# Centroid products of an attention kernel: float32 operands in place of two float32r parts

## The chip, the cores and the metric

The kernel runs on one core of a Trainium2 chip. The metric is the device time of the whole program in microseconds, the median of three runs. Five engines work side by side, each on its own list of instructions: PE (TensorE, matmuls; its weight loads are shown as PEld), DVE (VectorE), ACT (ScalarE), POOL (GpSimd), and SP, which only issues transfers here.

## The reference

Attention over 2 batches of 8 heads (768 positions, 64 wide) in which a query sees only the keys of its own cluster, then two feed-forward layers. What matters here is how a cluster is chosen:

```python
q_n = q / (norm(q) + 1e-6);  k_n = k / (norm(k) + 1e-6);  c_n = centroids / (norm(centroids) + 1e-6)
q_assign = argmax(einsum('bhsd,hcd->bhsc', q_n, c_n), axis=-1)      # 16 centroids per head
k_assign = argmax(einsum('bhsd,hcd->bhsc', k_n, c_n), axis=-1)
mask = q_assign[:, :, :, None] == k_assign[:, :, None, :]
attn = softmax(where(mask, q @ k.T / sqrt(64), -1e9));  x = attn @ v
x = g1(x @ w1_in) @ w1_out;  out = g2(x @ w2_in) @ w2_out           # 1536 tokens, 512 and 2048 wide
```

A query's length does not change which centroid wins, so the kernel normalises the centroids alone.

## The kernel before

Two heads make a pair; there are eight pairs, 0 to 7. Matmuls take float32r, a shortened float32, so the kernel splits each float32 value into a high part (rounded to float32r) and a low part (the rest) and adds the products of the parts.

The attention is a pipeline of slots, 24 for each pair. In a slot (`run_slot`) PE transposes three 128x128 blocks of the softmax numerators p into a PSUM tile pt (L527), makes half a row block of scores s (L475, L478), and multiplies earlier blocks with v (L545, L546). ACT copies pt into its high part phi (L530) and takes exponentials (L493). DVE takes row maxima nm (L484) and the low part plo of pt (L535), and only then is pt's PSUM bank free. Three PSUM banks (`ps_t`) serve pt and all other short-lived PSUM tiles in turn.

`prep_pair(i)` prepares pair i while pair i-1 is in its slots. Each `yield` ends its share of a slot. In its order:

- for q (s=0) and k (s=1) and each half hf: three transposes into ptq (L329), ACT copies ptq to SBUF as t32 (L337), and one slot later (`qk_parts`) POOL makes from t32 the high part th and the low part tl (L301, L302). For pairs 2 to 7 (`i >= NDVE`) t32 is a tile with two buffers, so that the third and fourth copy use the buffers of the first and second; pairs 0 and 1 write th directly.
- over four further slots the products with the centroids: for each block of 128 positions two matmuls, with th and with tl as the stationary operand, and 64 moving columns that hold the high and the low parts of the pair's centroids (L367, L368). One step of a slot is three blocks, so six matmuls.
- `sum_dots`, once for q and once for k: DVE adds the products with the two centroid parts and writes dots to SBUF (L356).
- then, a slot or more apart, the winner: maximum mx (L414), comparison eq (L416), a product on POOL (L418), and two more steps on DVE (L423, L425), which make a one-hot code in dots.

From about the middle of the attention on, `pump` adds one step of the conversion of the feed-forward weights every eighth slot (wx and w, L139 to L158, most of them on DVE). POOL's list in the slots of a preparation holds the parts of v (L439, L440), of the attention's result (L584, L585) and of t32, in an order fixed when the program is built. In slots 18 and on the order on PE, ACT, DVE and POOL is the order in which the code issues (`manual_schedule`); before that a scheduler orders it. The feed-forward layers follow, 2,304 matmuls of 512 columns.

Of the kernel before, what the change touches and what calls it, by code (L numbers as in the profile page):

```python
# [8 lines left out]
F32 = mybir.dt.float32  # L9
# [5 lines left out]
ALU = mybir.AluOpType  # L15
AX = mybir.AxisListType
PSUM = bass.MemoryType.PSUM

P = 128
# [8 lines left out]
NDVE = 2  # L28
# [4 lines left out]
def attention_moe_moe(  # L33
# [18 lines left out]
    nc = tc.nc  # L52
    B, H, S, D = q.shape
    C = centroids.shape[1]
    NT, DM = out.shape
    DFF = w1_in.shape[1]
    NJ = S // P
    HJ = NJ // 2
    HS = S // 2
    NPAIR = H // 2  # L60
# [33 lines left out]
    xh = cpool.tile([P, NPAIR, NT], F32R, name="xh")  # L94
    xl = cpool.tile([P, NPAIR, NT], F32R, name="xl")
    cn = cpool.tile([P, NPAIR, 2, 2, C], F32R, name="cn")

# [3 lines left out]
    def later(n, f, *args):  # L103
        due.setdefault(now[0] + n, []).append((f, args))
# [85 lines left out]
    with ExitStack() as actx:  # L190
# [42 lines left out]
        def centroid_setup(ct):  # L233
            sq = ct[:, 1]
            nc.vector.tensor_tensor(sq, ct[:, 0], ct[:, 0], ALU.mult)
            ss = ap.tile([P, 5], F32, tag="css", name="css")
            nc.vector.tensor_reduce(ss[:, 0:1], sq, AX.X, ALU.add)
            y = ss[:, 1:2]
            sq = nc.scalar.activation(y, ss[:, 0:1], AF.Sqrt)
            with tc.issue_after(ins(sq)):  # L240

                nc.scalar.activation(ss[:, 4:5], desc[:, 0:1], AF.Exp, scale=0.0)
            for _ in range(2):
                nc.vector.tensor_scalar(y, y, 1e-30, None, ALU.max)
                nc.vector.reciprocal(ss[:, 2:3], y)
                nc.vector.scalar_tensor_tensor(
                    ss[:, 3:4], ss[:, 0:1], ss[:, 2:3], y, ALU.mult, ALU.add)
                nc.vector.tensor_scalar(y, ss[:, 3:4], 0.5, None, ALU.mult)
            nc.vector.tensor_scalar(ss[:, 2:3], y, 1e-6, None, ALU.add)
            nc.vector.reciprocal(ss[:, 3:4], ss[:, 2:3])  # L250
            cd = ap.tile([P, HS], F32, tag="xt1", bufs=2, name="cd")[:, :P].rearrange(
                "p (r d) -> p r d", r=2)
            for r in range(2):
                nc.vector.tensor_scalar(cd[:, r], ct[:, 0], ss[:, 3:4], None, ALU.mult)
            nc.vector.memset(cn.bitcast(F32), 0.0)
            return cd

        def centroid_parts(cd):
            pc = ps_t.tile([P, HS], F32, tag="t", name="pc")
            mm = nc.tensor.transpose(pc[:, :P], cd.rearrange("p r d -> p (r d)"), ident)  # L260
            run_idle(NIDLE[1], ins(mm))
            pcv = pc[:, :P].rearrange("p (g h c) -> p g h c", h=2, c=C)
            for r in range(2):
                rows = slice(r * D, (r + 1) * D)
                nc.scalar.activation(cn[rows, :, 0, r], pcv[rows, :, r], AF.Copy)
                nc.vector.tensor_tensor(
                    cn[rows, :, 1, r], pcv[rows, :, r], cn[rows, :, 0, r].bitcast(F32),
                    ALU.subtract)

        prepped = {}  # L270

# [4 lines left out]
        def prep_pair(i):  # L276
# [7 lines left out]
            else:  # L284
# [2 lines left out]
            st = [[ap.tile([P, 2, S], F32R, tag=f"st{n}", bufs=3, name=f"st{n}_{i}_{h}")  # L287
                   for n in range(2)] for h in range(2)]
            prepped[i] = [None, st]

            def copy(dst, src):
                nc.sync.dma_start(dst.bitcast(F32), src.bitcast(F32))
# [31 lines left out]
            for s in range(2):  # L324
                sc = D ** -0.5 if s == 0 else 1.0
                for hf in range(2):
                    pt = ps_t.tile([P, HS], F32, tag="t", name=f"ptq{i}_{s}_{hf}")
                    for jj in range(HJ):
                        tr = nc.tensor.transpose(  # L329
                            pt[:, jj * P:(jj + 1) * P],  # L330
                            t[:, s, hf * HJ + jj].rearrange("p h d -> p (h d)"), ident)
                    cols = slice(hf * HS, (hf + 1) * HS)
                    if i < NDVE:
                        t32 = th[:, s, cols]
                    else:
                        t32 = ap.tile([P, HS], F32, tag="t32", bufs=2, name=f"t32_{i}_{s}_{hf}")
                    nc.scalar.activation(t32, pt, AF.Copy, scale=sc)  # L337
                    later(1, qk_parts, s, cols, t32, pt, sc)
                    yield
                later(1, stack, s)  # L340
                if i == 0 and s == 0:
                    with tc.issue_after(ins(tr)):
                        centroid_parts(cd)
                yield
# [13 lines left out]
                    pd.rearrange("p j t h c -> p j (h c) t"), AX.X, ALU.add)  # L358

            rhs = cn[:, hp].rearrange("p t h c -> p (t h c)")  # L360
            for s in range(2):
                pd = ps_t.tile([P, NJ, 2, 2, C], F32, tag="t", name=f"pd{i}_{s}")
                for j in range(NJ):
                    cols = slice(j * P, (j + 1) * P)
# [45 lines left out]
            else:  # L410
                dv = dots.rearrange("p j s h c -> p (j s h) c")
                mb = mx.unsqueeze(2).to_broadcast([P, G, C])
                yield
                nc.vector.tensor_reduce(mx, dv, AX.X, ALU.max)  # L414
                yield
                nc.vector.tensor_tensor(eq, dv, mb, ALU.is_ge)  # L416
                yield
                nc.gpsimd.tensor_tensor(  # L418
                    eq, eq, desc.unsqueeze(1).to_broadcast([P, G, C]), ALU.mult)
# [369 lines left out]
```

## Time and profile before

| | |
|---|---|
| three runs | 816.03 us median (815.66 to 819.19) |
| profiled execution | span 818.6 us from the first to the last instruction; no time of its own is listed |
| PE busy | 797.4 us, 97% of the span |
| PEld, DVE, ACT, POOL busy | 82%, 77%, 49%, 35% |
| attention, then feed-forward | to about 283 us, then 536 us |
| mean granted clock of TensorE | 0.991 |

The span is 0.6 us below the slowest of the three runs and 2.6 us above their median. A matmul's record begins when it starts to stream and its end is modelled, so that records overlap; how long the engine needs for one in a row of its kind is read from start to start.

### The profile page before, as it was taken

How to read it: one execution, taken by the hardware profiler on the slowest of the kernel's cores; microseconds unless marked ns; L12 is line 12 of the kernel's file. 1: busy time of each engine (PE TensorE's matmuls, PEld its weight loads, DVE VectorE, ACT ScalarE, POOL GpSimd, SP SyncE). 2: the span in 40 equal slices, each digit the busy share in tenths (PEclk: the TensorE clock that was granted, in tenths of full speed). 3: DMA queues.
4: the chain of work that ended last, by engine and by line, in shares of the span. 5: the costliest groups of instructions: out<-in, count | busy, mean ns of one | idle time of the engine just before them, and what ended most of it. 6: DMA issues, size and time to landing. Idle time of an engine off the chain costs nothing.

```text
span 818.6 us, 11285 instructions
## 1 busy us (share of the span) xinstructions
PE 797.4 (97%) x4042; PEld 670.6 (82%) x4042; DVE 629.7 (77%) x957; ACT 400.3 (49%) x762; POOL 282.6 (35%) x425
## 2 busy tenths in 40 slices
PE   8899999999999999999999999999999999999998
PEld 5789988889888877888888888888888888888886
DVE  6878978968899787777977777898876987755552
ACT  3688878767788665443434333323444233222220
POOL 3347558574674532222221112332231122111110
PEclk9999999988999999999999999999999999999999
DMA  7875553565440103213121313112122221000012
GB/s 155 192 147 121 134 126 88 119 154 108 97 89 32 52 2 103 92 63 103 52 91 64 102 52 104 52 54 100 52 70 86 61 86 59 1 1 0 14 50 91
DMA packets 48183, 65.97 MB, mean 81 GB/s; under 512 B 27904, under 2 KB 32640, under 8 KB 48128
## 3 DMA queue, kind: packets, MB, share of 16 engines
q1 hardware_dynamic: 47984, 65.22, 29.5%
q8 instruction: 32, 0.52, 0.3%
q14 instruction: 23, 0.19, 0.1%
q10 hardware_dynamic: 144, 0.03, 0.0%
HBM read 43.02 MB, written 3.15 MB: 56 GB/s over the span
## 4 chain that ended last, share of the span: by engine, by line
PE 76%; DVE 10%; POOL 6%; ACT 4%; issue 2%; DMA 1%; SPq 0%; POOLq 0%; ACTq 0%; DVEq 0%
PE y L699 11%; PE y L700 11%; PE y L701 11%; PE h L701 10%; PE h L699 10%; PE h L700 10%; PE pt L527 4%; DVE plo L535 3%; DVE nm L484 3%; PE s L475 2%; PE s L478 2%; PE o L546 2%; PE o L545 2%; ACT phi L530 1%; PE pd L368 1%
## 5 line engine op out<-in xcount | busy, mean ns | idle before, releaser
L657 POOL TENSOR_SCALAR gh<-g 128x512 fp32r<-128x512 f32 x96 | 71.5, 745 | 278.0 <-DVE g L688 157.4
L699 PE MATMUL h<-xh,w 128*128 128x512 f32 x384 | 151.4, 394 | 0.5 <-DVE g L674 0.5
L700 PE MATMUL h<-xl,w 128*128 128x512 f32 x384 | 151.4, 394 | 0.0
L701 PE MATMUL h<-xh,w 128*128 128x512 f32 x384 | 151.3, 394 | 0.0
L535 DVE TENSOR_TENSOR plo<-pt,phi 128x384 fp32r<-128x384 f32 x192 | 99.6, 547 | 16.6 <-ACT phi L530 15.8
L530 ACT ACTIVATE phi<-pt 128x384 fp32r<-128x384 f32 x192 | 93.2, 494 | 36.2 <-PE pt L527 34.4
L484 DVE TENSOR_REDUCE nm<-s 128x1 f32<-128x768 f32 x96 | 91.0, 948 | 19.8 <-PE s L478 18.8
L527 PE MATMUL pt<-ident,p 128*128 128x128 f32 x576 | 98.5, 279 | 7.8 <-DVE plo L535 5.8
L684 ACT ACTIVATE p<-h,mone 128x512 f32<-128x512 f32 x48 | 33.1, 690 | 130.0 <-DVE m L683 129.6
L493 ACT ACTIVATE p<-s,nm 128x768 f32<-128x768 f32 x96 | 86.6, 902 | 8.8 <-DVE nm L484 7.8
L661 DVE TENSOR_TENSOR gl<-g,gh 128x512 fp32r<-128x512 f32 x96 | 71.6, 746 | 20.0 <-POOL gh L657 15.3
L699 PEld LDWEIGHTS h<-xh,w 128*128 128x128 f32 x384 | 71.9, 187 | 18.4 <-DVE g L674 1.0
L701 PEld LDWEIGHTS h<-xh,w 128*128 128x128 f32 x384 | 71.8, 187 | 17.7
L527 PEld LDWEIGHTS pt<-ident,p 128*128 128x128 f32 x576 | 69.9, 141 | 20.0 <-issue 4.2
L700 PEld LDWEIGHTS h<-xl,w 128*128 128x128 f32 x384 | 71.9, 187 | 17.5
L475 PE MATMUL s<-st,st 128*128 128x384 f32 x192 | 81.6, 425 | 2.5 <-ACT p L493 2.3
L139 ACT ACTIVATE wx<-wraw 128x1024 f32<-128x1024 f32 x32 | 36.5, 1140 | 95.5 <-DMA wraw<-in_moe_w_out_dram 47.7
L699 PE MATMUL y<-gh,w 128*128 128x512 f32 x192 | 74.9, 390 | 1.3 <-POOL w L155 1.3
L700 PE MATMUL y<-gl,w 128*128 128x512 f32 x192 | 74.8, 390 | 0.0
L700 PE MATMUL y<-w,gh 128*128 128x512 f32 x192 | 74.8, 390 | 0.0
L699 PE MATMUL y<-w,gh 128*128 128x512 f32 x192 | 74.7, 389 | 0.0
L738 DVE TENSOR_TENSOR acc<-y,acc 128x512 f32<-128x512 f32 x72 | 49.2, 685 | 33.1 <-PE y L701 33.1
(120 smaller groups left out, 1636.3 us busy)
## 6 DMA issues: line engine op xcount, KB each, us to landing
wraw<-in_moe_w_in_dram SPq DMA_DIRECT2D x16, 1024.0 KB, 5.1
wraw<-in_moe_w_out_dram SPq DMA_DIRECT2D x16, 1024.0 KB, 4.9
st<-t SPq DMA_DIRECT2D x24, 192.0 KB, 4.3
st<-th SPq DMA_DIRECT2D x9, 384.0 KB, 4.0
st<-tl SPq DMA_DIRECT2D x18, 192.0 KB, 4.0
st<-th SPq DMA_DIRECT2D x18, 192.0 KB, 4.3
nat<-in_q_dram SPq DMA_DIRECT2D x8, 384.0 KB, 5.1
nat<-in_k_dram SPq DMA_DIRECT2D x8, 384.0 KB, 5.8
```

The costliest lines, as they stand in the source:

```text
L475: nc.tensor.matmul(s[:, step, :HS], qt[:, 0, cols], kt[:, 0, kc], start=True, stop=False)
L484: nc.vector.tensor_reduce(nm, s[:, :, :HS], AX.XY, ALU.max, negate=True)
L493: nc.scalar.activation(p, s[:, :, :HS], AF.Exp, bias=nm, accum_out=dens[u][:, jj, 0:1])
L527: nc.tensor.transpose(ps[:, jj * P:(jj + 1) * P], p[:, kt * P:(kt + 1) * P], ident)
L530: nc.scalar.activation(hi, ps, AF.Copy)
L535: nc.vector.tensor_tensor(lo, ps, hi.bitcast(F32), ALU.subtract)
L657: nc.gpsimd.tensor_scalar(hi, g, 1.0, 0.0, ALU.mult, ALU.add)
L661: nc.vector.tensor_tensor(lo, g, hi.bitcast(F32), ALU.subtract)
L699: nc.tensor.matmul(o, lh, rh, start=first, stop=False)
L700: nc.tensor.matmul(o, lh, rl, start=False, stop=False)
L701: nc.tensor.matmul(o, ll, rh, start=False, stop=last)
L738: nc.vector.tensor_tensor(a, po, a, ALU.add)
```

## The change

For pairs 2 to 7 the products with the centroids become float32 products: the stationary operand is t32 itself, the moving one is `cn32`, 32 columns of float32 centroids (high part plus low part). One matmul stands where two stood (72 where there were 144), all 12 blocks of q and k go into one PSUM tile pd32, and the sum of parts is not needed: mx and eq read pd32 from PSUM. t32 gets four buffers. `cn32` is cleared and filled once by POOL at the start. th and tl are still made; the scores need them. Pairs 0 and 1 are as before.

```diff
--- before.py
+++ after.py
@@ -94,6 +94,7 @@
     xh = cpool.tile([P, NPAIR, NT], F32R, name="xh")
     xl = cpool.tile([P, NPAIR, NT], F32R, name="xl")
     cn = cpool.tile([P, NPAIR, 2, 2, C], F32R, name="cn")
+    cn32 = cpool.tile([P, NPAIR, 2, C], F32, name="cn32")
 
 
 
@@ -253,6 +254,7 @@
             for r in range(2):
                 nc.vector.tensor_scalar(cd[:, r], ct[:, 0], ss[:, 3:4], None, ALU.mult)
             nc.vector.memset(cn.bitcast(F32), 0.0)
+            nc.gpsimd.memset(cn32, 0.0)
             return cd
 
         def centroid_parts(cd):
@@ -266,6 +268,15 @@
                 nc.vector.tensor_tensor(
                     cn[rows, :, 1, r], pcv[rows, :, r], cn[rows, :, 0, r].bitcast(F32),
                     ALU.subtract)
+            later(6, centroid_sum)
+
+        def centroid_sum():
+
+            for r in range(2):
+                rows = slice(r * D, (r + 1) * D)
+                nc.gpsimd.tensor_tensor(
+                    cn32[rows, :, r], cn[rows, :, 0, r].bitcast(F32),
+                    cn[rows, :, 1, r].bitcast(F32), ALU.add)
 
         prepped = {}
 
@@ -287,6 +298,8 @@
             st = [[ap.tile([P, 2, S], F32R, tag=f"st{n}", bufs=3, name=f"st{n}_{i}_{h}")
                    for n in range(2)] for h in range(2)]
             prepped[i] = [None, st]
+
+            t32s = {}
 
             def copy(dst, src):
                 nc.sync.dma_start(dst.bitcast(F32), src.bitcast(F32))
@@ -333,7 +346,8 @@
                     if i < NDVE:
                         t32 = th[:, s, cols]
                     else:
-                        t32 = ap.tile([P, HS], F32, tag="t32", bufs=2, name=f"t32_{i}_{s}_{hf}")
+                        t32 = ap.tile([P, HS], F32, tag="t32", bufs=4, name=f"t32_{i}_{s}_{hf}")
+                    t32s[(s, hf)] = t32
                     nc.scalar.activation(t32, pt, AF.Copy, scale=sc)
                     later(1, qk_parts, s, cols, t32, pt, sc)
                     yield
@@ -358,7 +372,19 @@
                     pd.rearrange("p j t h c -> p j (h c) t"), AX.X, ALU.add)
 
             rhs = cn[:, hp].rearrange("p t h c -> p (t h c)")
-            for s in range(2):
+            pd32 = None
+            if i >= NDVE:
+
+                pd32 = ps_t.tile([P, NJ, 2, 2 * C], F32, tag="t", name=f"pd{i}")
+                for s in range(2):
+                    for j in range(NJ):
+                        jj = j % HJ
+                        nc.tensor.matmul(
+                            pd32[:, j, s], t32s[(s, j // HJ)][:, jj * P:(jj + 1) * P],
+                            cn32[:, hp].rearrange("p h c -> p (h c)"), start=True, stop=True)
+                        if jj == HJ - 1:
+                            yield
+            for s in range(2 if i < NDVE else 0):
                 pd = ps_t.tile([P, NJ, 2, 2, C], F32, tag="t", name=f"pd{i}_{s}")
                 for j in range(NJ):
                     cols = slice(j * P, (j + 1) * P)
@@ -410,10 +436,11 @@
             else:
                 dv = dots.rearrange("p j s h c -> p (j s h) c")
                 mb = mx.unsqueeze(2).to_broadcast([P, G, C])
+                dp = dv if pd32 is None else pd32.rearrange("p j s (h c) -> p (j s h) c", c=C)
                 yield
-                nc.vector.tensor_reduce(mx, dv, AX.X, ALU.max)
+                nc.vector.tensor_reduce(mx, dp, AX.X, ALU.max)
                 yield
-                nc.vector.tensor_tensor(eq, dv, mb, ALU.is_ge)
+                nc.vector.tensor_tensor(eq, dp, mb, ALU.is_ge)
                 yield
                 nc.gpsimd.tensor_tensor(
                     eq, eq, desc.unsqueeze(1).to_broadcast([P, G, C]), ALU.mult)
```

Where the instructions stand now, at three places of the preparation of pair 4 (its copies t32, its products, its winner). The rows are in the order of the engine; in brackets the engines whose signal an instruction waits for; a wait that an earlier one implies is not listed. Lines of the changed kernel are higher by 13 to 27.

ACT before, the four copies t32 (`t_4_s_hf`) with the copies phi and exponentials p between them:

```order
L337 ACTIVATE t_4_0_0_1586<-ptq_0_0_1582 128x384 [waits PE_49]
L530 ACTIVATE phi_3_1592<-pt_3_1588 128x384 [waits PE_49,Activation_49]
L337 ACTIVATE t_4_0_1_1603<-ptq_0_1_1599 128x384 [waits PE_49]
L530 ACTIVATE phi_4_1611<-pt_4_1607 128x384 [waits PE_49,Activation_49]
L493 ACTIVATE p_1624,den_1537<-s_1560,nm_1605 128x768 [waits DVE_49]
L530 ACTIVATE phi_5_1635<-pt_5_1631 128x384 [waits PE_49,Activation_49]
L337 ACTIVATE t_4_1_0_1653<-ptq_1_0_1649 128x384 [waits PE_49,Activation_49,Pool_49]
L530 ACTIVATE phi_0_1661<-pt_0_1657 128x384 [waits PE_49]
L493 ACTIVATE p_1672,den_1671<-s_1614,nm_1655 128x768 [waits DVE_49]
L337 ACTIVATE t_4_1_1_1682<-ptq_1_1_1678 128x384 [waits PE_49,Activation_49,Pool_49]
L530 ACTIVATE phi_1_1688<-pt_1_1684 128x384 [waits PE_49]
L530 ACTIVATE phi_2_1703<-pt_2_1699 128x384 [waits PE_49]
```

and in the changed kernel:

```order
L351 ACTIVATE t_4_0_0_1560<-ptq_0_0_1556 128x384 [waits PE_49]
L557 ACTIVATE phi_3_1566<-pt_3_1562 128x384 [waits PE_49,Activation_49]
L351 ACTIVATE t_4_0_1_1577<-ptq_0_1_1573 128x384 [waits PE_49]
L557 ACTIVATE phi_4_1585<-pt_4_1581 128x384 [waits PE_49,Activation_49]
L520 ACTIVATE p_1598,den_1511<-s_1534,nm_1579 128x768 [waits DVE_49]
L557 ACTIVATE phi_5_1609<-pt_5_1605 128x384 [waits PE_49,Activation_49]
L351 ACTIVATE t_4_1_0_1627<-ptq_1_0_1623 128x384 [waits PE_49]
L557 ACTIVATE phi_0_1635<-pt_0_1631 128x384 [waits PE_49]
L520 ACTIVATE p_1646,den_1645<-s_1588,nm_1629 128x768 [waits DVE_49,Pool_49]
L351 ACTIVATE t_4_1_1_1656<-ptq_1_1_1652 128x384 [waits PE_49]
L557 ACTIVATE phi_1_1662<-pt_1_1658 128x384 [waits PE_49,Activation_49]
L557 ACTIVATE phi_2_1677<-pt_2_1673 128x384 [waits PE_49,Activation_49]
```

The order is the same. The third and the fourth copy waited for POOL and now wait for PE alone. The second p lists POOL now, for its buffer den, which POOL read for the last time some 24 slots earlier; before, the copy's wait implied it.

PE before, the first step of products (`pd`) and the transposes and scores around it:

```order
L546 MATMUL o_1617<-plo_5_1636,vv_991 128x384
L367 MATMUL pd_0_1727<-cn,th_1576 128x64 [waits Activation_49]
L368 MATMUL pd_0_1727<-cn,tl_1577 128x64 [waits Pool_49]
L367 MATMUL pd_0_1727<-cn,th_1576 128x64
L368 MATMUL pd_0_1727<-cn,tl_1577 128x64
L367 MATMUL pd_0_1727<-cn,th_1576 128x64
L368 MATMUL pd_0_1727<-cn,tl_1577 128x64
L527 MATMUL pt_3_1734<-ident,p_1538 128x128 [waits DVE_49,PE_49]
L527 MATMUL pt_3_1734<-ident,p_1567 128x128
L527 MATMUL pt_3_1734<-ident,p_1624 128x128
L475 MATMUL s_1706<-st_2_1_541,st_2_1_540 128x384
L478 MATMUL s_1706<-st_2_1_541,st_2_1_540 128x384
```

and in the changed kernel:

```order
L573 MATMUL o_1591<-plo_5_1610,vv_980 128x384
L382 MATMUL pd_1701<-cn_103,t_4_0_0_1560 128x32 [waits Activation_49]
L382 MATMUL pd_1701<-cn_103,t_4_0_0_1560 128x32 x2
L554 MATMUL pt_3_1705<-ident,p_1512 128x128 [waits DVE_49,PE_49]
L554 MATMUL pt_3_1705<-ident,p_1541 128x128
L554 MATMUL pt_3_1705<-ident,p_1598 128x128
L502 MATMUL s_1680<-st_2_1_545,st_2_1_544 128x384
L505 MATMUL s_1680<-st_2_1_545,st_2_1_544 128x384
L382 MATMUL pd_1701<-cn_103,t_4_0_1_1577 128x32 x3
```

Three rows stand where six stood, in the same slot; the waits for POOL on the products of this and the next step are gone. The wait of the first row, for ACT, stays, as does that of pt for DVE.

DVE before, from the first sum of parts to the comparison:

```order
L356 TENSOR_REDUCE dots_1726<-pd_0_1727 128x6x32
L484 TENSOR_REDUCE nm_1798<-s_1758 128x1 [waits PE_49]
L535 TENSOR_TENSOR plo_5_1784<-pt_5_1779,phi_5_1783 128x384 [waits DVE_49,Activation_49]
L535 TENSOR_TENSOR plo_0_1805<-pt_0_1800,phi_0_1804 128x384 [waits DVE_49,Activation_49]
L356 TENSOR_REDUCE dots_1726<-pd_1_1772 128x6x32
L414 TENSOR_REDUCE mx_1818<-dots_1726 128x24 [waits DVE_49]
L484 TENSOR_REDUCE nm_1832<-s_1807 128x1 [waits PE_49]
L535 TENSOR_TENSOR plo_1_1825<-pt_1_1820,phi_1_1824 128x384 [waits Activation_49]
L535 TENSOR_TENSOR plo_2_1839<-pt_2_1834,phi_2_1838 128x384 [waits Activation_49]
L416 TENSOR_TENSOR eq_1819<-dots_1726,mx_1818 128x384 [waits DVE_49]
```

and in the changed kernel:

```order
L511 TENSOR_REDUCE nm_1758<-s_1726 128x1 [waits PE_49]
L562 TENSOR_TENSOR plo_5_1747<-pt_5_1742,phi_5_1746 128x384 [waits DVE_49,Activation_49]
L562 TENSOR_TENSOR plo_0_1765<-pt_0_1760,phi_0_1764 128x384 [waits DVE_49,Activation_49]
L441 TENSOR_REDUCE mx_1777<-pd_1701 128x24
L511 TENSOR_REDUCE nm_1791<-s_1767 128x1 [waits PE_49]
L562 TENSOR_TENSOR plo_1_1784<-pt_1_1779,phi_1_1783 128x384 [waits DVE_49,Activation_49]
L562 TENSOR_TENSOR plo_2_1798<-pt_2_1793,phi_2_1797 128x384 [waits DVE_49,Activation_49]
L443 TENSOR_TENSOR eq_1778<-pd_1701,mx_1777 128x384 [waits DVE_49]
```

The two sums of parts (L356) are gone; mx and eq (now L441, L443) stand at the places of L414 and L416 and read pd. PSUM banks: before, pd_0 and pd_1 each held a bank from their first product to their sum; now pd32 holds one from its first product to eq.

## Rows read from the trace of the kernel before

**Rows 1.** The page, busy time of the engines and count of their instructions.

```profile
PE 797.4 (97%) x4042; PEld 670.6 (82%) x4042; DVE 629.7 (77%) x957; ACT 400.3 (49%) x762; POOL 282.6 (35%) x425
```

**Rows 2.** Stretches: length, busy PE, PEld, DVE, ACT, POOL, granted clock, DMA share, GB/s.

```profile
19.00:179.00 160.00, 151.79 (x1037) 139.06 (x1036) 135.39 (x238) 123.48 (x278) 99.56 (x154) 1.00 0.58 129
179.00:190.00 11.00, 11.00 (x47) 10.82 (x46) 5.96 (x12) 3.97 (x9) 1.82 (x4) 0.54 1.04 244
```

**Rows 3.** Timeline of PE, pair 7: start, duration, what; in brackets idle and releaser.

```profile
216.56 0.34 PE L546 MATMUL o<-plo,vv 128*128 128x384 f32 x1
216.74 0.19 PE L367 MATMUL pd<-cn,th 128*128 128x64 f32 x1
...
216.88 0.28 PE L367 MATMUL pd<-cn,th 128*128 128x64 f32 x1
...
217.33 0.55 PE L527 MATMUL pt<-ident,p 128*128 128x128 f32 x3
217.63 0.42 PE L475 MATMUL s<-st,st 128*128 128x384 f32 x1
```

**Rows 4.** Waits in the attention: us in total, times, longest.

```profile
ACT t L337 <- POOL tl L302: 5.4, 4, 1.6
...
ACT t L337 <- POOL t L302: 3.1, 3, 1.4
```

**Rows 5.** Timeline, first product steps: PE in pairs 3 and 4, DVE in 3.

```profile
77.20 0.33 PE L546 MATMUL o<-plo,vv 128*128 128x384 f32 x1
...
78.66 0.52 PE L527 MATMUL pt<-ident,p 128*128 128x128 f32 x3 [0.21 <-DVE plo L535]
...
108.78 0.33 PE L546 MATMUL o<-plo,vv 128*128 128x384 f32 x1
...
110.10 0.52 PE L527 MATMUL pt<-ident,p 128*128 128x128 f32 x3 [0.21 <-DVE plo L535]
...
77.96 1.02 DVE L535 TENSOR_TENSOR plo<-pt,phi 128x384 fp32r<-128x384 f32 x2 [0.81 <-ACT phi L530]
```

**Rows 6.** Timeline, pair 5: PE, then DVE.

```profile
140.71 0.33 PE L546 MATMUL o<-plo,vv 128*128 128x384 f32 x1
...
142.56 0.52 PE L527 MATMUL pt<-ident,p 128*128 128x128 f32 x3 [0.21 <-DVE plo L535]
...
140.57 0.90 DVE L143 TENSOR_SCALAR wx<-wx 128x1024 int32<-128x1024 int32 x1
141.85 1.02 DVE L535 TENSOR_TENSOR plo<-pt,phi 128x384 fp32r<-128x384 f32 x2 [0.39 <-ACT phi L530]
```

**Rows 7.** Timeline, pair 6: ACT, then PE, then DVE.

```profile
172.51 0.49 ACT L337 ACTIVATE t<-ptq 128x384 f32<-128x384 f32 x1 [1.63 <-POOL tl L302]
...
172.02 0.34 PE L546 MATMUL o<-plo,vv 128*128 128x384 f32 x1
173.06 0.55 PE L329 MATMUL ptq<-ident,nat 128*128 128x128 f32 x3 [0.70 <-ACT t L337]
...
177.34 0.52 PE L527 MATMUL pt<-ident,p 128*128 128x128 f32 x3 [0.26 <-DVE plo L535]
...
175.20 1.52 DVE L158 TENSOR_TENSOR w<-wx,w 128x1024 fp32r<-128x1024 f32 x1
176.65 1.01 DVE L535 TENSOR_TENSOR plo<-pt,phi 128x384 fp32r<-128x384 f32 x2
```

**Rows 8.** Timeline after pair 5's products: DVE, then PE.

```profile
149.16 0.55 DVE L356 TENSOR_REDUCE dots<-pd 128x192 f32<-128x384 f32 x1
149.74 0.55 DVE L414 TENSOR_REDUCE mx<-dots 128x24 f32<-128x384 f32 x1
...
151.07 1.01 DVE L535 TENSOR_TENSOR plo<-pt,phi 128x384 fp32r<-128x384 f32 x2
...
150.74 0.49 PE L527 MATMUL pt<-ident,p 128*128 128x128 f32 x3
...
151.77 0.52 PE L527 MATMUL pt<-ident,p 128*128 128x128 f32 x3 [0.18 <-DVE plo L535]
```

## The prediction

> **What bounds the kernel now.** I read the busy times of the page first: PE is busy for 797.4 of 818.6 us [rows 1], so only what PE does or waits for can move the time much. The stretches come next. The change lies in the attention, and in its 160 us from 19 to 179 PE is busy 151.8 us, DVE 135.4, ACT 123.5, POOL 99.6, all at full clock; then follow 11 us at a mean granted clock of 0.54, between the levels of 2.4 and 1.2 GHz [rows 2]. So PE leads, DVE is close behind, and there are some microseconds of waiting to look for. The timeline of PE shows them: five of the six preparations that the change touches (pairs 3 to 7) have a late transposition pt right behind the first product step. In the undisturbed step the last product with v (L546) starts at 216.56, the products at 216.74 and pt at 217.33: 0.77 us from L546 to pt [rows 3]. In pair 3 it is 78.66 - 77.20 = 1.46 us, in pair 4 110.10 - 108.78 = 1.32 us [rows 5].
>
> The waits tell where this begins. ACT's copies t32 waited 5.4 + 3.1 = 8.5 us for POOL's low parts [rows 4]: the third copy needs the buffer that POOL still reads. ACT works in order, so phi behind the copy is late, then plo on DVE, then the PSUM bank that pt needs. PE's wait is therefore put down to DVE, though POOL caused it.
>
> **The products themselves.** One now takes 0.1125 us (the last four of a step, 216.88 to 217.33), although its 64 columns stream in far less: 384 columns of the product before took 0.18 us, 216.56 to 216.74 [rows 3]. So what sets the pace is the change of the 128 stationary columns, which each matmul brings. Each float32 product does the work of two old ones. No row shows one. Bounds: if it needed one load and one pass, as a float32 transposition does (three in 0.30 us, 217.33 to 217.63), 72 products would take 72 x 0.10 against 144 x 0.1125 now, 7.2 - 16.2 = -9.0 us. If it needed four loads, 72 x 0.45 = 32.4, +16.2 us. I take two loads with a matmul each, and so no change: the built program holds 4,042 weight loads and 4,042 matmuls, as many as before [rows 1], so that 72 products stand as 144 loads and 144 matmuls. The moving side agrees: a float32 transposition streams 128 columns in 0.10 us, where float32r streams 384 in 0.18, 0.06 for 128; float32 columns take nearly twice as long, and 32 of them take what 64 took. So half the matmul rows in the listing buy PE nothing.
>
> The Trainium skill, "FP8 and Floating Point Precision", section "TensorE Precision Notes", says that true FP32 takes four passes through the array, one for each pairing of high and low halves. Read as four loads, its sum would be 16.2 us more; read as two loads whose matmul streams both halves of the moving operand, it is mine. The transposition row fits the second reading for the moving side, and no row here shows the loads.
>
> **The copies.** With four buffers the third and fourth copy wait for PE alone, and the 8.5 us of ACT's waiting go. What PE gets of it is less, because DVE is late next:
>
> - Pairs 3 and 4: pt comes 0.69 and 0.55 us earlier (1.46 and 1.32 less 0.77). In pair 3 DVE sat idle 0.81 us for phi ahead of the plo that held pt [rows 5], so that plo can come as much earlier, and nothing takes the wait's place; pair 4 has no weight step either. 1.24 us.
> - Pair 5: 142.56 - 140.71 = 1.85, so 1.08 us late. But a weight step (L143, 0.90 us from 140.57) stands on DVE ahead of plo. It ends at 141.47. The two plo take 1.02 us together, the first about 0.55 (an estimate; they overlap a little), so it ends at 142.02 [rows 6]. pt follows 0.15 us later, as at 151.77 after a first plo begun at 151.07 [rows 8]: at 142.17, a gain of 0.39. Pair 7 has the same rows 71.4 us later: 0.39.
> - Pair 6: the transpositions of q and k at 173.06 go back to 172.02 + 0.18 = 172.20 (ACT's 1.63 us for POOL was in their way), 0.86 us. On DVE L158, 1.52 us long, moves with them from 175.20 to 174.34 and ends at 175.86, the first plo at 176.41, and pt comes at 176.56 where it was 177.34: 0.78 [rows 7].
> - Pair 2: a scheduler has moved its products by a few rows; the copies have little to gain there. I take 0, with pair 4's 0.55 us to either side.
>
> Together 1.24 + 0.78 + 0.78 = 2.8 us. If DVE's weight steps did not hold pt, pairs 5 and 7 would give 1.08 each, 0.69 more, and pair 6 up to its L158, 1.52 more: 2.9 us, the good end.
>
> **The sums of parts.** Twelve on DVE go. The first of each pair lies before an idle stretch and gives nothing. The second, 149.16 to 149.74, stands at the head of a stretch in which DVE works without a pause and PE waits for plo (151.77, [rows 8]): 0.58 us. Against it stands the longer hold of the bank: pd32 keeps it until eq, so that the transposition at 150.74 has only two banks. It waits for the plo that comes at 151.07, now 150.49, done at 151.04, so that pt starts at 151.19, 0.45 us late. That takes the place of the wait at 151.77, about as long: on PE the stretch itself gains next to nothing, 0.05 us in each of pairs 2 to 4 as an estimate. In pairs 5 to 7 weight steps keep DVE behind for longer, so the 0.58 us reach PE at the next wait, less about 0.13 for the row maximum whose scores come later: 3 x 0.45. Together 1.5 us. If the wait for the bank and the old one both stay, it is 0.
>
> **Nothing else.** mx takes 0.55 us from SBUF and the sum took 0.55 from PSUM [rows 8], so reading pd32 costs nothing; eq has the same size. POOL's clearing and two additions come once, at the start; POOL is the least busy engine, 35% [rows 1], and PE wants their result in pair 2 only. One load of k on SP moves behind four transfers; it is needed a pair later.
>
> **The sum.** 2.8 + 1.5 = 4.3 us. Its rows come from an execution with a span of 818.6, 2.6 above the median of 816.03; I take it from the median: 811.7 us. Own range 808.8 (the 2.9 us more) to 814.0 (nothing from the sums, 2 us from the copies).
>
> **Rivals.**
>
> A, the clock does not fall. The 11 us at 0.54 cost 11 x 0.46 = 5.1 us [rows 2]. They begin 1.7 us after the last of pair 6's late starts on PE (177.34, [rows 7]), and these shrink. For it: pairs 3 to 5, with smaller waits, lie in the stretch at full clock [rows 2]. Against it: pair 6 still waits over a microsecond by my own count, and the median may hold less of the fall than the profile. 818.6 - 5.1 - 4.3 = 809.2 by the span, 806.7 by the median; 808.
>
> B, the waits come back. DVE, busy for 85% of the attention, holds PE wherever POOL did, and the longer held bank eats the rest. For it: pairs 5 to 7 above. Against it: the idle 0.81 us of pair 3. No gain or one of 1 us: 815.5.
>
> C, the product is dear: four loads, 0.45 us, at each of 72 products on PE, which leads. 811.7 + 16.2 = 827.9. It turns the forecast into a loss from 4.3 / 72 = 0.06 us more a product. Against it: the count of loads.
>
> D, the product is cheap: the load is as short as a transposition's and only one counts. 811.7 - 9.0 = 802.7.
>
> **Chances.** Forecast 0.50, A 0.20, B 0.16, C 0.08, D 0.06. A measurement of this kernel tells from no change what differs by over about 0.5%, 4.1 us: below 811.95 is faster, above 820.1 slower. The forecast lies at that edge, 0.26 faster and 0.24 the same; A and D are faster, B the same, C slower. Faster 0.52, same 0.40, slower 0.08. The range takes in the forecast's, most of A and B: 806.8 to 816.3.
>
> **What would show it.** ACT's copies t32 no longer wait for POOL; L546 to pt in the first step near 0.8 us in pairs 3 and 4, and in pairs 5 to 7 still ended by plo behind a weight step. A product step that takes 0.6 us as before: 144 records of weight loads and a pace of 0.11 us. A step of 1.3 us is C, of 0.3 D. The stretch around 179 to 190 at clock 1.0 is A. Waits of pt for plo one slot earlier than at 151.77 show the bank. Wrong would be a time outside the range, or the right time with the copies still waiting.

## The result: 809.5 us, 0.8 to 1.1% faster

The changed kernel takes 809.47 us (median of 4, 809.46 to 809.51), the kernel before 817.61 (median of 4, 815.66 to 821.18). The ratio is 0.9887, 95% interval 0.9858 to 0.9916. In a second set the changed kernel had 809.21 (6, 809.03 to 811.26) against 816.08 (15, 815.42 to 821.59): 0.9917 (0.9899 to 0.9935). The forecast was 811.7 in a range of 806.8 to 816.3, so 2.2 us too high. Two of the four executions of before in the first set are 3.5 and 5.5 us above its shortest, which helps the first ratio; shortest against shortest it is 0.8% in both sets.

Two sizes have to be kept apart. Every run lists its time beside its span, and the time is 1.8 us longer (815.33 and 813.5, 809.03 and 807.3). The profiled execution of before, 818.6 us long, thus took about 820.4 (an estimate) and was one of the longest. Between the profiles lie 10.9 us; between the shortest executions 815.42 - 809.03 = 6.4. The 4.5 us between the two are in the main the fall of the clock that the profile of before shows after 179 us [rows 2] (4.4 in the table below): about one execution in five of that kernel is longer by more than 3 us (below).

The profile after: busy time of the engines, against [rows 1], then the stretches of [rows 2] (length, busy PE, PEld, DVE, ACT, POOL, granted clock, DMA share, GB/s).

```profile
PE 789.1 (98%) x4042; PEld 665.8 (82%) x4042; DVE 623.6 (77%) x945; ACT 400.4 (50%) x762; POOL 282.4 (35%) x428
```

```profile
19.00:179.00 160.00, 153.64 (x1072) 143.69 (x1071) 134.53 (x235) 126.40 (x284) 101.40 (x157) 1.00 0.60 136
179.00:190.00 11.00, 10.65 (x71) 9.63 (x70) 10.53 (x20) 9.94 (x23) 5.11 (x9) 1.00 0.71 142
```

In the same 160 us PE gets through 1,072 matmuls where it did 1,037, and as many matmul records as before stand on the whole page. The half clock after 179 us is gone from this execution.

ACT's waits for its copies t32, in the attention, against [rows 4] (us in total, times, longest), before and after: the waits for POOL are gone, and one row is left.

```profile
ACT t L337 <- PE ptq L329: 5.7, 4, 2.9
...
ACT t L351 <- PE ptq L342: 7.4, 8, 2.9
```

The waits for the transpositions that the copies read grew by 1.7 us.

The timeline of PE: the first steps of products of pairs 3, 4, 5 and 6, against [rows 5 to 7], and last a step that nothing delays (pair 6's third, where [rows 3] has one of pair 7).

```profile
76.87 0.33 PE L573 MATMUL o<-plo,vv 128*128 128x384 f32 x1
77.05 0.75 PE L382 MATMUL pd<-cn,t 128*128 128x32 f32 x6
77.63 0.53 PE L554 MATMUL pt<-ident,p 128*128 128x128 f32 x3
...
107.36 0.33 PE L573 MATMUL o<-plo,vv 128*128 128x384 f32 x1
107.53 0.75 PE L382 MATMUL pd<-cn,t 128*128 128x32 f32 x6
108.12 0.52 PE L554 MATMUL pt<-ident,p 128*128 128x128 f32 x3
...
138.11 0.33 PE L573 MATMUL o<-plo,vv 128*128 128x384 f32 x1
138.29 0.75 PE L382 MATMUL pd<-cn,t 128*128 128x32 f32 x6
139.45 0.52 PE L554 MATMUL pt<-ident,p 128*128 128x128 f32 x3 [0.41 <-DVE plo L562]
...
170.68 0.33 PE L573 MATMUL o<-plo,vv 128*128 128x384 f32 x1
170.85 0.75 PE L382 MATMUL pd<-cn,t 128*128 128x32 f32 x6
172.49 0.52 PE L554 MATMUL pt<-ident,p 128*128 128x128 f32 x3 [0.89 <-DVE plo L562]
...
175.21 0.75 PE L382 MATMUL pd<-cn,t 128*128 128x32 f32 x6
175.80 0.52 PE L554 MATMUL pt<-ident,p 128*128 128x128 f32 x3
```

From 175.21 to 175.80 is 0.59 us for three float32 products, the time of six products before (216.74 to 217.33). The records say x6: each product left two. From L573 to pt is 0.76 us in pairs 3 and 4; it was 1.46 and 1.32. In pairs 5 and 6 it is 1.34 and 1.81: PE still waits there, and plo holds it.

DVE at pair 5's first step, two slots behind pair 5's products, and at pair 6's first step; then PE behind pair 5's products, two slots on and three slots later, against [rows 8].

```profile
137.98 0.86 DVE L144 TENSOR_SCALAR wx<-wx 128x1024 int32<-128x1024 int32 x1
138.76 1.01 DVE L562 TENSOR_TENSOR plo<-pt,phi 128x384 fp32r<-128x384 f32 x2
...
147.30 1.01 DVE L562 TENSOR_TENSOR plo<-pt,phi 128x384 fp32r<-128x384 f32 x2
148.23 0.55 DVE L443 TENSOR_TENSOR eq<-pd,mx 128x384 f32<-128x384 f32 x1
...
170.54 1.33 DVE L159 TENSOR_TENSOR w<-wx,w 128x1024 fp32r<-128x1024 f32 x1
171.79 1.01 DVE L562 TENSOR_TENSOR plo<-pt,phi 128x384 fp32r<-128x384 f32 x2
```

```profile
147.38 0.34 PE L573 MATMUL o<-plo,vv 128*128 128x384 f32 x1
147.99 0.52 PE L554 MATMUL pt<-ident,p 128*128 128x128 f32 x3 [0.27 <-DVE plo L562]
...
150.94 0.34 PE L573 MATMUL o<-plo,vv 128*128 128x384 f32 x1
151.60 0.52 PE L554 MATMUL pt<-ident,p 128*128 128x128 f32 x3 [0.33 <-DVE plo L562]
```

In both first steps a weight step (L144, L159) stands ahead of plo. At 147.99 is a wait that before did not have at this slot: 0.61 us from L573 to pt instead of 0.18. The wait one slot later (151.77 in [rows 8], 0.35 us with another 0.19 behind it) is gone.

The wait at 151.60, 0.66 us from L573 to pt, stands behind a weight step on DVE and was 1.06 before. In pair 4 the weight step behind the sums stands on ACT (L139), ahead of the exponential p that the third transposition of a pt needs: it came 0.62 us late before, and 0.20 after. The rows of before, pair 5 and then pair 4:

```profile
154.28 0.34 PE L546 MATMUL o<-plo,vv 128*128 128x384 f32 x1
155.34 0.52 PE L527 MATMUL pt<-ident,p 128*128 128x128 f32 x3 [0.72 <-DVE plo L535]
...
120.36 1.16 ACT L139 ACTIVATE wx<-wraw 128x1024 f32<-128x1024 f32 x1
...
122.84 0.33 PE L527 MATMUL pt<-ident,p 128*128 128x128 f32 x1 [0.46 <-ACT p L493]
```

**Where the 10.8 us of the attention went.** The second matmul of the scores (L478, now L505) runs 192 times in the same order in both kernels, so subtracting its n-th start in one trace from that in the other gives what PE has gained up to each slot, and the slots at which the number changes. It is 0.14 at the first and 10.77 behind the last change:

| place | us gained |
|---|---|
| pair 2, all of it | 0.16, and 0.14 at a transposition later |
| first product steps of pairs 3, 4, 5, 7 | 0.69, 0.55, 0.52, 0.51 |
| pair 6: transpositions of q and k, first product step | 0.92, 0.20 |
| two slots behind the products, pairs 3, 4, 5, 7: new wait, old wait gone | -0.46 + 0.59 = 0.13 each |
| four to five slots behind, pairs 4, 5, 6, 7: the wait behind a weight step | 0.42, 0.40, 0.40, 0.41 |
| the stretch at half clock, and what of it came back | 4.79 - 0.42 |

These sum to 10.2, and steps under 0.04 us make up the other 0.4. Without the clock's row they are 5.8, or 6.3 with the small steps, beside 6.4 between the shortest executions.

### The profile page after: what moved, and what is told of

Read it like the earlier page. It is cut to its first block, busy times and chain, and to the rows that moved or that the text cites. A ratio compares the mean times of both kernels' runs of the same rounds, so it can differ in the third digit from the quotient of the medians.

```text
span 807.7 us, 11308 instructions
## 1 busy us (share of the span) xinstructions
PE 789.1 (98%) x4042; PEld 665.8 (82%) x4042; DVE 623.6 (77%) x945; ACT 400.4 (50%) x762; POOL 282.4 (35%) x428
## 4 chain that ended last, share of the span: by engine, by line
PE 85%; DVE 7%; ACT 3%; issue 2%; POOL 1%; DMA 1%; SPq 0%; ACTq 0%; DVEq 0%; POOLq 0%
PE y L726 11%; PE y L727 11%; PE y L728 11%; PE h L727 10%; PE h L728 10%; PE h L726 10%; PE pt L554 6%; PE s L502 3%; PE s L505 3%; PE o L573 3%; PE o L572 3%; DVE plo L562 2%; PE pd L382 2%; DVE nm L511 2%; PE ptq L342 1%
## 5 line engine op out<-in xcount | busy, mean ns | idle before, releaser
L511 DVE TENSOR_REDUCE nm<-s 128x1 f32<-128x768 f32 x96 | 91.3, 951 | 21.4 <-PE s L505 19.3
L554 PE MATMUL pt<-ident,p 128*128 128x128 f32 x576 | 96.8, 276 | 7.5 <-DVE plo L562 6.2
```

The costliest lines, as they stand in the source:

```text
L511: nc.vector.tensor_reduce(nm, s[:, :, :HS], AX.XY, ALU.max, negate=True)
L554: nc.tensor.transpose(ps[:, jj * P:(jj + 1) * P], p[:, kt * P:(kt + 1) * P], ident)
```

## The experiments

Each was timed with the kernel before on the same chip. Shortest executions are compared where a size of about a microsecond matters, since the clock falls for part of the executions of nearly every kernel. Code is cut to the lines that change.

**The copies alone** (the kernel before, t32 with four buffers).

```diff
-tag="t32", bufs=2
+tag="t32", bufs=4
```

> The kernel before with four buffers for t32 and nothing else. Theory 1 (slot by slot, the copies alone gave PE 0.69 us in pair 3, 0.55 in 4, 0.52 in 5, 1.12 in 6, 0.51 in 7, 3.4 together, and the fall of the clock after pair 6 follows from pair 6's late starts): 3.4 us below an execution of the kernel before without a fall (815.7), so 812.3, all executions within 0.3 us of each other, clock 1.0 from 179 to 190, the copies wait no longer for POOL. Theory 2 (the prediction's 2.8 us, and the clock falls for other reasons): 812.9 in the best execution, others up to 5 us longer, the stretch at half clock still in the profile.

812.09 us the shortest of 8 (median 812.50) against 815.33 the shortest of 25 (median 815.96): 3.24 less; ratio of all 0.995 (0.9932 to 0.9968). By the starts of the scores pairs 3 to 7 gave 0.67, 0.53, 0.48, 1.14 and 0.49 us, 3.3 together, so the sizes in the table are the copies'. Theory 1 had these right. Its "within 0.3 us of each other" was wrong: two of eight took 2.0 us more. The timeline of PE in this kernel:

```profile
139.23 0.34 PE L546 MATMUL o<-plo,vv 128*128 128x384 f32 x1
...
140.61 0.52 PE L527 MATMUL pt<-ident,p 128*128 128x128 f32 x3 [0.44 <-DVE plo L535]
...
149.81 0.52 PE L527 MATMUL pt<-ident,p 128*128 128x128 f32 x3 [0.18 <-DVE plo L535]
150.28 0.45 PE L475 MATMUL s<-st,st 128*128 128x384 f32 x1
```

Pair 5's wait for plo behind its first products is that of the changed kernel (1.38 us from L546 to pt, 1.34 there), while the wait of the kernel before two slots behind the products is unchanged, in its old slot.

**The sums alone** (two buffers stay; 32 moving columns, into one tile; the low parts of the centroids are left out).

```diff
+rhs32 = cn[:, hp, 0].rearrange("p h c -> p (h c)")
+pd32 = ps_t.tile([P, NJ, 2, 2 * C], F32, tag="t", name=f"pd{i}")
...
+nc.tensor.matmul(o, th[:, s, cols], rhs32, start=True, stop=False)
+nc.tensor.matmul(o, tl[:, s, cols], rhs32, start=False, stop=True)
...
-for s in range(2):
+for s in range(2 if i < NDVE else 0):
...
-nc.vector.tensor_reduce(mx, dv, AX.X, ALU.max)
+nc.vector.tensor_reduce(mx, dp, AX.X, ALU.max)
```

> The kernel before with th and tl as stationary operands still (144 matmuls), but moving only the 32 columns of the high centroid parts into one tile, maximum and comparison from that tile, no sums of parts; it leaves out the low parts of the centroids. Two buffers for t32 stay. Theory 1 (the twelve sums gave PE 2.3 us, 0.13 in each pair and 0.40 more in pairs 4 to 7): 2.3 us below before, 813.4 without a fall of the clock, to 819 with one, since pair 6's late starts stay. Theory 2 (prediction's size): 814.2. Rival (the longer held bank eats it): 815.7, no change.

813.14 us the shortest of 12 (median 813.62), 2.19 less; ratio 0.9975 (0.9957 to 0.9992). By the starts of the scores 0.12 in each of pairs 3, 4, 5 and 7 and 0.39 to 0.42 more in pairs 4 to 7. The wait for the longer held bank is here as in the changed kernel, with th and tl as operands (PE, pair 4):

```profile
117.53 0.33 PE L559 MATMUL o<-plo,vv 128*128 128x384 f32 x1
118.15 0.52 PE L540 MATMUL pt<-ident,p 128*128 128x128 f32 x3 [0.28 <-DVE plo L548]
```

**Both, without the float32 operands** (the two edits above together).

> The kernel before with four buffers for t32, moving only the 32 columns of the high centroid parts, one tile and no sums of parts (the low parts of the centroids are left out): all of the change but the float32 operands, 144 float32r products. Theory 1 (the float32 products themselves cost and give nothing, 0.59 us a step either way): within 0.4 us of the changed kernel, 809.0 to 809.6. Rival (the two parts alone, 3.2 and 2.2 us in the best executions, add up to 5.4, and the rest of the 6.3 is the float32 products'): 810.0 to 810.3.

809.79 us the shortest of 6 (median 810.27); ratio 0.9912 (0.9895 to 0.993), the changed kernel's within the intervals. From the first score matmul to the first of the feed-forward layers, a stretch that the start of the program doesn't touch, it takes 249.70 us, the changed kernel 249.13 (second profile). A step of six float32r products takes 0.584 to 0.589 us here, a step of three float32 products 0.584 to 0.589 there. So the operands bring nothing in the steps themselves. Theory 1's range of times was missed (809.79 against 809.6 at most), and the median lies in the rival's; but in the stretch the two kernels are 0.6 us apart, where the rival wanted 0.9. Of the 0.6, 0.25 lies at the start of pair 2's preparation, 0.14 at the later transposition of the table, and the rest in small pieces; how the operands would bring these is not shown.

**One load for each block** (the changed kernel; the low parts of q, k and the centroids are left out).

```diff
-pd32[:, j, s], t32s[(s, j // HJ)][:, jj * P:(jj + 1) * P],
-cn32[:, hp].rearrange("p h c -> p (h c)"), start=True, stop=True)
+pd32[:, j, s], th[:, s, j * P:(j + 1) * P],
+cn[:, hp, 0].rearrange("p h c -> p (h c)"), start=True, stop=True)
```

> The changed kernel with float32r products of th and the high centroid parts, one per block: 72 matmuls of 32 columns with one weight load each; it leaves out the low parts of q, k and the centroids in the choice of a cluster. Theory 1 (a float32 product is two loads with a matmul each and the loads set the pace of 0.1 us): a product step takes 0.30 to 0.34 us where it takes 0.59, 24 steps give 6.0 to 7.0 us on PE; where pt is held by plo (pairs 5 to 7, three steps) it comes back as waiting, about 0.8: 803 to 804.5. Rival (the float32 product is as short as one float32r product): the steps stay at 0.59, 809.5.

804.05 us the shortest of 5 (median 804.19); ratio 0.9845 (0.9823 to 0.9866). A step takes 0.25 us (PE):

```profile
201.69 0.40 PE L382 MATMUL pd<-cn,th 128*128 128x32 f32 x3
201.95 0.55 PE L554 MATMUL pt<-ident,p 128*128 128x128 f32 x3
```

The blocks and the moving columns are those of the changed kernel; only the halves differ, three a step in place of six, and (0.586 - 0.251) / 3 = 0.112 us for each is the pace read in [rows 3]. In pairs 3 to 7 the 15 second to fourth steps give 0.335 us each, 5.0; the first steps of pairs 3 and 4 give 0.2 each, those of pairs 5 to 7, where plo holds pt, nothing; pair 2's four give 1.15 together, and 0.1 to 0.2 a pair is lost behind the products: 249.13 - 243.46 = 5.7 us by the stretch from the first score to the feed-forward layers. Theory 1 holds; only its step of 0.30 to 0.34 us was too long.

**Pair 6's copies alone**, for the clock.

```diff
-tag="t32", bufs=2
+tag="t32b" if i == 6 and s == 1 else "t32", bufs=2
```

> The kernel before with buffers of their own for the third and fourth copy of pair 6 alone. Theory 1: the late starts of pair 6 come before the fall of the clock and make it; here they go, 1.1 us of waiting with them, and the clock stays up: 814.6, executions within 0.3 us, pairs 3, 4, 5, 7 as before. Theory 2: what makes the clock fall is not in pair 6 (load of the whole chip, an earlier stretch): 814.6 to 820, scattered as before, half clock from about 178 on.

Theory 1 fell. The shortest of 12 is 814.64, 0.7 below 815.33, but the others reach 820.72 (median 816.48; ratio 1.0, 0.9982 to 1.0018), with a mean granted clock of 0.990 to 1.000, lower in the longer ones. By the starts of the scores pair 6 gave its 0.92 and 0.22 us all the same (in the profile of this run the first score comes 0.5 us later than before). The profiled execution is one without the fall, so that the longer ones are known by their times and mean clocks alone. Its stretch behind pair 6, and there PE's first products, which still wait for plo:

```profile
179.00:190.00 11.00, 10.36 (x70) 9.38 (x70) 9.24 (x18) 8.39 (x19) 5.18 (x10) 1.00 1.08 252
```

```profile
175.47 0.28 PE L369 MATMUL pd<-cn,tl 128*128 128x64 f32 x1
176.61 0.52 PE L528 MATMUL pt<-ident,p 128*128 128x128 f32 x3 [0.86 <-DVE plo L536]
```

**The changed kernel again.**

> The changed kernel again, for its scatter. Theory 1 (what makes the clock fall for some microseconds between 179 and 190 in executions of the kernel before is rarer here): at least 9 of 10 executions within 0.5 us of 809.5. Theory 2 (the fall comes as often as before, and four executions were too few to meet it): a third of the executions 1 to 5 us longer.

The shortest is 809.03; four of six lie within 0.25 us of it, two are 2.0 and 2.2 longer at a clock of 0.996; with the first set eight of ten are close, where theory 1 wanted nine. In this profile the program's first 17 us ran at full clock, and its first score matmul came at 17.4 us; in the kernel with both edits the mean there was 0.82 and it came at 19.3 (stretches, columns as above):

```profile
0.00:17.00 17.00, 13.64 (x70) 7.93 (x72) 10.77 (x40) 7.05 (x14) 7.38 (x41) 1.00 0.81 160
```

```profile
0.00:17.00 17.00, 14.12 (x62) 8.25 (x63) 10.38 (x39) 6.63 (x14) 6.59 (x38) 0.82 0.85 166
```

In the run below with one weight step in slot 15, whose start is the changed kernel's, the mean was 0.82 as well and the first score came at 19.6. So there are two falls. One at the program's start costs about 2 us, and most of these kernels have executions that are so much longer. The other costs more, 4.4 us in the profile of before. More than 3 us above the shortest of their set are 10 of the 55 executions of before, 4 of 12 with pair 6's buffers alone and 3 of 12 with the sums alone, 17 of 79; of the 60 executions of kernels in which every copy has a buffer of its own, none (the highest 2.8). What all of the first have is the wait of copies for POOL in pairs 3, 4, 5 and 7. This goes together in the counts; that the waits make the clock fall is not shown, nor which of them it needs.

**The bank sooner, by time** (the changed kernel; mx and eq one slot earlier each) **and by a copy on ACT.**

```diff
-yield
+if pd32 is None:
+    yield
 nc.vector.tensor_reduce(mx, dp, AX.X, ALU.max)
 yield
 nc.vector.tensor_tensor(eq, dp, mb, ALU.is_ge)
 yield
+if pd32 is not None:
+    yield
```

> The changed kernel with maximum and comparison one slot earlier each, so that pd32 gives its bank back a slot earlier. Theory 1 (the wait of 0.38 to 0.44 us for plo, two slots behind the last products of each of six pairs, is there because pt has two banks while pd32 holds the third): six waits of 0.43 us go or halve, 807 to 808.2. Rival (DVE is simply behind at that place, whoever holds the bank): the waits move a slot and keep their size, 809.3 to 809.8.

```diff
+if pd32 is not None:
+    nc.scalar.activation(dv, dp, AF.Copy)
+    dp = dv
 yield
 nc.vector.tensor_reduce(mx, dp, AX.X, ALU.max)
```

> The changed kernel with a copy of pd32 to SBUF on ACT (0.5 us) right behind the last products; maximum and comparison read the copy, and the bank is free after the copy. Theory 1 (bank): the six waits of 0.43 us go, but six phi come up to 0.5 us later on ACT: 807 to 809. Rival (DVE is behind, the bank is no cause): no gain and the later phi, 809.5 to 811.

Both are slower than the changed kernel: 810.88 the shortest of 5 (0.9935, 0.9917 to 0.9954) and 812.99 of 8 (0.9962, 0.9949 to 0.9974). In both the six waits of 0.43 go, as theory 1 said, and in both one comes at the next slot that is larger. With the earlier mx and eq it is the old one, 0.35 + 0.19; behind it pairs 4 and 6 lose their 0.4 again. DVE and PE behind pair 3's products:

```profile
84.67 0.56 DVE L444 TENSOR_TENSOR eq<-pd,mx 128x384 f32<-128x384 f32 x1
85.14 0.95 DVE L514 TENSOR_REDUCE nm<-s 128x1 f32<-128x768 f32 x1
86.01 1.01 DVE L565 TENSOR_TENSOR plo<-pt,phi 128x384 fp32r<-128x384 f32 x2
```

```profile
86.70 0.52 PE L557 MATMUL pt<-ident,p 128*128 128x128 f32 x3 [0.18 <-DVE plo L565]
87.17 0.44 PE L505 MATMUL s<-st,st 128*128 128x384 f32 x1
```

With the copy on ACT (0.49 us at 84.79) phi is later as well, the wait is 0.54 + 0.19, and pairs 4 to 7 each lose their 0.4 again. The rival had the direction, DVE is behind in these slots whoever holds the bank, but both times came out above its ranges. What the held bank costs by itself is not shown: each edit also makes plo late on its own, by eq ahead of it on DVE or by the copy ahead of phi on ACT.

**The weight steps elsewhere** (the changed kernel; three steps in 24 slots each time).

```diff
-if 64 <= slot < 192 and slot % 8 == 5:                # 5, 13, 21
+if 64 <= slot < 192 and slot % 8 == 7:                # first run
+if 64 <= slot < 192 and slot % 24 in (5, 15, 21):     # second
+if 64 <= slot < 192 and slot % 24 in (5, 15, 17):     # third
```

> The changed kernel with the weight steps of the attention two slots later (slots 7, 15, 23 of a pair's 24 in place of 5, 13, 21), so that the one that stood ahead of the first products falls between the second and the third step of products. Theory 1 (a weight step on DVE ahead of plo is what now holds pt behind the first products of pairs 5, 6, 7: 0.58, 1.05 and 0.62 us, while the longer slots of the products leave DVE time): these three waits go, and those of 0.2 to 0.5 behind slot 21 change places: 807 to 808. Rival (DVE has no slack anywhere in these slots): the waits move along with the weight steps and keep their sum, 809.5 to 810.5.

> The changed kernel with only the weight step of slot 13 moved, to slot 15 (steps in slots 5, 15, 21 of 24). Theory 1 (from the run with all steps moved: the waits behind the first products gave back 0.57, 0.44 and 0.61 us in pairs 5, 6, 7, while the steps moved from slots 5 and 21 cost more): 1.6 us less, 807.4 to 807.8. Rival (the weight step between the products makes plo late for what comes after the products, in slots 18 to 21): 809 to 810.

> The changed kernel with weight steps in slots 5, 15 and 17 of 24: both near the products, where a slot of PE is 0.59 us longer. Theory 1 (DVE has 4 x 0.59 = 2.4 us of slack in these four slots, two steps of about 1.1 us fit): the waits of 0.20 to 0.49 us three slots after the bank's go too: 806.2 to 807. Rival (the second step holds the plo of slot 18, and the wait there is longer than the one saved): 807.5 to 809.

All three steps two slots later: 811.66 the shortest of 7, slower (0.9954, 0.9937 to 0.9971). The waits behind the first products went as expected, 0.57, 1.04 and 0.61 us, but in pair 6 0.60 came back two slots on, and new ones of up to 1.26 came behind the steps' new slots 7 and 23. With the step of slot 13 alone in slot 15 the shortest of 5 is 807.81, the median 808.69 (0.9893, 0.9874 to 0.9912); its stretch from first score to feed-forward is 247.62, 1.5 less than the changed kernel's. By that stretch it beats both kernels; the medians, from different chips, do not tell it from the changed kernel. Theory 1 had the sum, not its parts: 0.57 and 0.58 us came in pairs 5 and 7 and 0.65 behind pair 7, but in pair 6 1.04 came and 1.12 went again, since the weight step, now between the products, took 2.03 us. DVE and POOL there, and the same step on DVE in pair 7:

```profile
174.46 2.03 DVE L159 TENSOR_TENSOR w<-wx,w 128x1024 fp32r<-128x1024 f32 x1
176.42 1.01 DVE L562 TENSOR_TENSOR plo<-pt,phi 128x384 fp32r<-128x384 f32 x2
...
236.41 1.22 DVE L159 TENSOR_TENSOR w<-wx,w 128x1024 fp32r<-128x1024 f32 x1
```

```profile
173.80 0.51 POOL L314 TENSOR_SCALAR th<-t 128x384 fp32r<-128x384 f32 x1
174.40 1.02 POOL L315 TENSOR_TENSOR tl<-t,th 128x384 fp32r<-128x384 f32 x1
175.39 1.48 POOL L314 TENSOR_SCALAR th<-t 128x384 fp32r<-128x384 f32 x1
```

The third run (808.40 the shortest of 6; 0.9899, 0.9879 to 0.9919) came out by its rival: the second step near the products cost 0.92 us in each of pairs 5 to 7, about what it saved, and the feed-forward layers became 2.1 us longer, from their first matmul to the end (542.81 for 540.71).

## Why the prediction was right, and where its sizes were off

The products: right. Bounds of -9.0 and +16.2 us, 0 taken, 0 measured: 0.585 us a step on both sides, and the profile has two matmul records for each float32 product, as it has 4,042 matmuls in all. Cheap products (rival D) would have been worth 5.7 us, by the run with one load, not 9. The Trainium skill's rule of four passes ("FP8 and Floating Point Precision", "TensorE Precision Notes") does not show as four loads: rival C's step of 1.3 us is nowhere in the profile. The support from the moving side was weak: the 0.10 us of a float32 transposition, read as the time of its columns, is near the 0.112 us that any half of a product takes with its load, so it need not be the columns.

The copies: right in mechanism, 2.8 us forecast and 3.3 measured. Pairs 3 and 4 came out as read (0.69 and 0.55). In pairs 5 to 7 plo behind a weight step held pt, as said, but for a little less: 0.52 and 0.51 us gained for 0.39 (in pair 5 the first plo began 0.65 us behind the last product with v, where the sum had 0.76), and 1.12 for 0.78. In pair 6 the weight step L159 took 1.33 us where the sum had carried over the 1.52 of before (there L158, [rows 7]). Pair 2, taken at 0, gave 0.16 and 0.14; the second came with neither part alone nor with both, so it belongs to something that only the changed kernel has.

The sums of parts and the bank: the step that failed in size, 1.5 us forecast and 2.2 measured. The exchange of the old wait for one a slot earlier is there, 0.46 for 0.59, so 0.13 a pair and not 0.05. The larger part is pair 4, which the prediction put among the pairs without a weight step behind the sums. It has one, on ACT and not on DVE: L139, 1.16 us at 120.36 in the trace of before, ahead of p, and the wait of 0.62 us at 122.84 became 0.20. The 0.45 us each of pairs 5 to 7 were 0.40, 0.40 and 0.41.

The base: the forecast took 4.3 us from the median of 816.03, which held 0.2 to 0.7 us of lower clock; executions at clock 1.0 take 815.3 to 815.8. And the 818.6 us of the span were not 2.6 above the median but, as a time, 4.4. The prediction left that open ("the median may hold less of the fall than the profile"), and what rival A wanted did happen: no long fall in ten executions of the changed kernel. But it moves the median little, because four in five executions of before don't have it either. Its cause by pair 6's late starts, for which the rival argued, is refuted as far as times and clocks go by the run with pair 6's buffers: without those late starts 4 of 12 executions were still over 3 us longer. The time of 809.5 by itself lies nearer to A's 808 than to the forecast; that it is the forecast's mechanism is shown by the executions at clock 1.0 on both sides, 6.4 us apart, and by the runs with one part each. Of the 2.2 us that the forecast was too high, 0.5 are the copies, 0.7 the sums, some 0.6 the base, and the rest pair 2 and steps too small to place.

## What to carry to other kernels

Ask of a removed wait what is late next, slot by slot: here it was the same plo, behind a weight conversion or a comparison on an engine that is busy for 85% of the stretch, and the estimate for each place held to some 0.4 us, pair 4's weight step on ACT included, which had been overlooked. Counting instructions in a listing says little on TensorE: 72 float32 products cost what 144 float32r products did, and the time came from a buffer count and twelve reductions. And where the executions of a kernel scatter, lay the shortest ones side by side, or align two traces on an instruction that both run in the same order: a profiled execution can hold over four microseconds that most others don't.

## What the runs showed of the hardware

A float32 matmul of 128 stationary and 32 moving columns is two matmuls in the trace and costs what two of float32r do: 0.59 us for three of the one or six of the other, 0.112 for each half more.

DVE and POOL slowed each other where both read operands in SBUF. With the step of slot 13 in slot 15, the weight step L159 took 1.22 us in pair 7, where POOL had nothing to do for its whole length, and 2.03 in pair 6 beside tl and th, of which th took 1.48 instead of 0.51 while tl kept its 1.02. The Trainium skill ("GPSIMD Engine Reference", "Specifications") names contention with DVE instructions that have two SBUF inputs; this subtraction has two, and the trace agrees. Moving a step on DVE thus needs a look at POOL's list at its new place.
